# Scores of chunks three to six as products of 64 rows and columns, with k's halves swapped in four heads

## The chip, the cores and the metric

The kernel runs on one core of one Trainium2 chip. The metric is the device time of one execution in microseconds (us). A core has five engines that run their own instruction streams and wait for one another by semaphores: PE (TensorE, matrix products; PEld is its weight load), DVE (VectorE), ACT (ScalarE), POOL (GpSimd) and SP (SyncE), which here issues all DMAs, in order. DMAs run on 16 DMA engines.

## The reference

An mLSTM cell on q, k, v of 4 batches, 8 heads, 768 steps and 40 values per head, then a feed-forward block of 320 to 2,048 to 320 with an exact GELU between:

```python
for t in range(S):
    m_new = np.maximum(f_gate[:, :, t] + m, i_gate[:, :, t])
    f_stab, i_stab = np.exp(f_gate[:, :, t] + m - m_new), np.exp(i_gate[:, :, t] - m_new)
    C = f_stab * C + i_stab * einsum('bhd,bhe->bhde', vt, kt)
    n = f_stab * n + i_stab * kt
    h_tilde = einsum('bhde,bhe->bhd', C, qt)
    y[:, :, t] = sigmoid(o_gate[:, :, t]) * h_tilde / np.maximum(np.abs((n * qt).sum(-1)), 1.0)
h = x @ w_in                      # x: y as 3072 tokens of 320
out = (0.5 * h * (1 + erf(h / sqrt(2)))) @ w_out
```

(The gate's factors are cut here: each holds for a batch and a head.)

## The kernel before

**Tiling.** The 768 steps are cut in six chunks of 128 (`c` = 0 to 5 in the code, chunk one to six in words). Within a chunk, the cell is attention-like: for each batch `b` and head `h`, scores `k q` of 128 key steps (on partitions) by 128 query steps are multiplied by weights `W` (an exponential of gate sums, zero where a key lies after its query), and the product with `v` gives the part of this chunk; what came before enters by a state that is carried from chunk to chunk. A finished chunk of 4 batches is 512 tokens, and goes through the feed-forward block while the next chunk's cell is worked on.

**One cell's steps** (class `Cell`, from L368). `mask` (L378): POOL's affine_select puts 1e30 where the query step comes before the key step, in a tile `W` that a DMA has filled with the gates' running maximum (`load_M`, L154, from the DRAM tile `M_d`). `weights` (L384): ACT takes the exponential for each head, with `aT`, a column per head and key step, as bias; 1e30 becomes zero. `turn_k` and `turn_q`: DVE turns k and q, loaded in blocks by `load_blocks` (L138), into `kT` and `qT`; two heads lie on the two halves of the partitions. `scores` (L469): for each of four pairs of heads and each half `hip`, one fp32 product of 64 rows (40 in use), 128 columns of `kT` and 128 of `qT`, into the PSUM bank of that half (L479); then DVE multiplies each bank into `W` (L482). `carry_two` (L522): products with the state (L531, 64x64 tiles) and, but for the last chunk, what this chunk adds to it (L538, with `kb` and `vw`; `vw` is v times `ewT`, made on POOL at L466). `values` (L564): `W` times `vb` (L573).

`kb` and `vb` hold k and v with key steps on partitions (`load`, L129, one DMA each per cell, L135); from chunk three on `load` is called with 1 and 3, for k and v alone, and with 3 and 4 for the output gate. `aT` and `ewT` come from the gates at the start (`gates_turned`, L215, called by `later_gates`, L276, for the later chunks).

**Order.** It is written out by hand. `FRONT` is a string of steps for the first two chunks and the conversion of the weights; `DOWN` is one for each later chunk's cell among the second products of the chunk before. From chunk three on the cell's scores come in pairs of batches: scores of two batches, `carry_two`, values of two, with feed-forward products between (L768 and L779 up, L844 down). In `FRONT`, the weights arrive as double-precision bits in 26 pieces: `fetch` (L310) loads one on SP, `conv_one` (K, L322) and `conv_two` (J, L340) convert it on DVE and ACT, and `conv_two` fetches the piece four places on, once its buffer is free. `F` is one row of the first chunk's down products (L821), which needs its piece of `w_out`. Letters B are `load_M`, X is `turn_y` (which loads ahead for the cell four places on), R is `split_x`.

Of the kernel before, what the change touches and what calls it, by code (L numbers as in the profile page):

```python
# [9 lines left out]
F32 = mybir.dt.float32  # L10
F32R = mybir.dt.float32r
BF16 = mybir.dt.bfloat16
U32 = mybir.dt.uint32
AF = mybir.ActivationFunctionType
OP = mybir.AluOpType

P = 128
# [11 lines left out]
    I2 O0 g0 L0 P0 L1 E k1 t0 P1 P2 k7 w0 N k2 w1 O1 K L2 Q s0 O3 w2 q D k2 d P3 t1 w3 c0 L3 J v0 t2 K K y0 s1 I7 v1  # L29
    I8 O2 J g1 L4 I5 c1 K I1 I2 y1 s2 x0 t3 B4 O4 B5 g2 J x1 s3 v2 c2 L5 y2 H T0 x2 G0 v3 g3 c3 K y3 M1 J L6 J A x3  # L30
    M0 K W0 O7 K A O6 O5 J M2 W1 S0 C0 K J J T1 U U K L7 V0 K T2 J J A G2 K G1 Y0 W2 S1 K M3 C1 A J S2 J K W3 K V1 C2
    Y1 T3 J J U U S3 V2 K K J G3 J Y2 C3 X0 K V3 J K F J F K K B8 F J K F F J K F F F R0 X1 J J K F J F K X2 F J K F
    J Y3 K F R1 J F Z B9 B10 F X3 R2 Z R3 F"""
DOWN = """
    M0 Z M1 W0 F L3 F B3 W1 Z Z F S0 Z S1 K2 C0 M2 Z G0 G1 G2 G3 V0 Z V1 W2 Z F Q2 K3 Q3 Y0 M3 D3 F F W3 F Z S2 S3
# [4 lines left out]
def kernel(  # L40
# [16 lines left out]
    nc = tc.nc  # L57

    B, H, S, D = q.shape
    L = P  # L60
    NCH = S // L
    NP = H // 2
# [7 lines left out]
    R = P // 2  # L70
# [13 lines left out]
    dram = ctx.enter_context(tc.tile_pool(name="dram", bufs=1, space=bass.MemoryType.DRAM))  # L84
# [12 lines left out]
    ident = const.tile([P, P], F32, name="ident")  # L97
# [3 lines left out]
    aT = const.tile([P, NCH, BH], F32, name="aT")  # L101
    ewT = const.tile([P, NCH - 1, BH], F32, name="ewT")
# [19 lines left out]
    f_sb = gates.tile([BH, NCH, L], F32, name="f_sb")  # L122
    i_sb = gates.tile([BH, NCH, L], F32, name="i_sb")
    M_d = dram.tile([NCH - 1, BH, L], F32, name="M_d")

    def out_of(n):
        return ob[n % NLD].rearrange("p (h d) -> p h d", d=D)

    def load(n, first=0, end=4):  # L129

        if n >= NCH * B:
            return
        c, b = divmod(n, B)
        for src, dst in ((q, qb), (k, kb), (v, vb), (o_gate, None))[first:end]:
            nc.sync.dma_start(out=dst[turn_of(n)][:, :, 0:D] if dst else out_of(n),  # L135
                              in_=src[b, :, c * L:(c + 1) * L, :].rearrange("h p d -> p h d"))

# [12 lines left out]
    def turn_of(n):  # L150

        return n % NLD if n < 2 * B else (n - 2 * B) % NQ
# [19 lines left out]
    for t in vb:  # L172
# [4 lines left out]
                            pattern=[[0, P]], channel_multiplier=1)  # L177
    nc.gpsimd.memset(beyond, 0.0)
    nc.gpsimd.affine_select(out=beyond, in_=beyond, compare_op=OP.is_ge, fill=1.0e30, base=0, pattern=[[1, L]],
                            channel_multiplier=-1)  # L180
# [15 lines left out]
    for j in range(3):  # L196
        m = slice(BH * j, BH * (j + 1))
# [17 lines left out]
    def gates_turned(*parts):  # L215

        for src, dst in parts:
            n = dst.shape[1]
            pg = ps_tr.tile([P, n, BH], F32, name="pg", tag="tr")
            for c in range(n):  # L220
                nc.tensor.transpose(pg[:, c, :], src[:, c, :], ident[0:BH, 0:BH])
            nc.vector.tensor_copy(out=dst, in_=pg)

    def gates_of(c0, c1):

        flat = lambda t: t[:, c0:c1].rearrange("p c l -> p (c l)")
        nc.vector.tensor_tensor_scan(out=flat(bl), data0=flat(keep), data1=flat(f_sb), initial=0.0,
                                     op0=OP.mult, op1=OP.add)
        nc.vector.tensor_tensor(out=a[:, c0:c1], in0=i_sb[:, c0:c1], in1=bl[:, c0:c1], op=OP.subtract)
        for c in range(c0, c1):  # L230
            nc.vector.tensor_tensor_scan(out=M[:, c], data0=a[:, c], data1=a[:, c], initial=m0[:, c:c + 1],
                                         op0=OP.max, op1=OP.max)
            if c + 1 < NCH:
                nc.vector.tensor_tensor(out=m0[:, c + 1:c + 2], in0=bl[:, c, L - 1:L], in1=M[:, c, L - 1:L],
                                        op=OP.add)
# [11 lines left out]
    def decays_turned(e0, e1, g0, g1):  # L247
        e, g = slice(e0, e1), slice(g0, g1)
        gates_turned((ew[:, e], ewT[:, e]), (gg[:, g], gT[:, g]))

    def decays_last(g0, g1):
        g = slice(g0, g1)
        pd = ps_tr.tile([P, g1 - g0, BH], F32, name="pd", tag="tr")
        nc.tensor.matmul(pd.rearrange("p c n -> p (c n)"), last, gT[:, g].rearrange("p c n -> p (c n)"),
                         start=True, stop=True)
        nc.vector.tensor_copy(out=dec[:, g], in_=pd)
# [27 lines left out]
    for name, w in (("in", moe_w_in), ("out", moe_w_out)):  # L284
        rows, cols = w.shape
# [66 lines left out]
    halves = (slice(0, R), slice(R, P))  # L352
# [7 lines left out]
    def unread(bank):  # L360
        for _ in range(idle[0]):
            nc.tensor.matmul(bank, ident, ident, start=True, stop=True, skip_group_check=True)
        idle[0] = 0
# [4 lines left out]
    class Cell:  # L368
# [9 lines left out]
        def mask(self, b):  # L378

            t = Mb[self.c * B + b]  # L380
            nc.gpsimd.affine_select(out=t, in_=t, compare_op=OP.is_ge, fill=1.0e30, base=0,  # L381
                                    pattern=[[0, H], [1, L]], channel_multiplier=-1)

        def weights(self, b):  # L384

# [83 lines left out]
        def scores(self, b):  # L469
            n = self.c * B + b  # L470
            kT, qT = self.kT.pop(b), self.qT[b]

            pool, tag = (ps_tr, "tr") if self.c > 0 and b % 2 else (ps_mm, "a")
            ps = [pool.tile([P, NP, L], F32, name="ps", tag=tag) for hip in range(2)]
            unread(ps[0][:, 0, :])
            for p in range(NP):
                for hip in range(2):
                    r = halves[hip]
                    nc.tensor.matmul(ps[hip][:, p, :], kT[r, p, :], qT[r, p, :], start=True, stop=True)  # L479
            for hip in range(2):  # L480
                w = W[n].rearrange("p (m two) t -> p m two t", two=2)[:, :, hip, :]
                nc.vector.tensor_tensor(out=w, in0=ps[hip], in1=w, op=OP.mult)  # L482
# [75 lines left out]
        def read(self, b):  # L558

            self.reads.append(b)  # L560
            if self.c > 1 and self.reads.count(b) == 2:
                load(self.c * B + b + NQ, 1, 3)
# [77 lines left out]
    w_sums, parts, fars, w_hi, w_lo, w_mid = [], {}, [], [], [], {}  # L640
# [86 lines left out]
    def first_up_steps(h):  # L727

        def step(k):
            ups.append((len(ups) + len(tags_next) % 2, (2 * k, 2 * k + 2, HT * h, HT * h + HT)))  # L730
            if len(ups) == 2:
                first_up()

        return [lambda k=k: step(k) for k in range(HF // 2)]
# [170 lines left out]
    def in_turn(steps):  # L905
        todo = list(steps)
        return lambda: todo.pop(0)() if todo else None

    def cell_steps(c, letters, before=None):
# [8 lines left out]
    n_pieces = range(len(pieces))  # L918
    steps = dict(P=fetch, L=lambda n: load(n, 0, 2), O=lambda n: load(n, 2, 4), B=load_M, E=second_gates, N=later_gates,
                 I=keep_clock, k=warm, D=lambda: decays_turned(0, 2, 0, 1), Q=lambda: decays_turned(2, NCH - 1, 1, NCH - 1),  # L920
                 d=lambda: decays_last(0, 1), q=lambda: decays_last(1, NCH - 1),
                 A=in_turn(first_up_steps(0)), U=in_turn(first_up_steps(1)), F=in_turn(first_down_steps(first_g)),
                 K=in_turn(lambda i=i: conv_one(i) for i in n_pieces), H=products_begin,
                 J=in_turn(lambda i=i: conv_two(i) for i in n_pieces), Z=split_weight)
    steps |= cell_steps(0, "mwgtscvyx") | cell_steps(1, "MWGTSCVYXR")
    play(FRONT, steps)
    for c in range(1, NCH):
# [6 lines left out]
        products, late = down_steps(c, g)  # L934
# [32 lines left out]
```

## Time and profile before

| what | before |
|---|---|
| median of 3 runs | 484.1 us (484.06 to 484.65) |
| profiled execution, its own time | 484.47 us |
| its span (first to last instruction) | 482.7 us |
| PE busy | 473.8 us (98%) |
| DVE busy | 346.4 us (72%) |
| ACT busy | 222.3 us (46%) |
| POOL busy | 69.5 us (14%) |
| granted TensorE clock | 1.0 |
| scores of two batches, chunks three to six | 1.99 us, eight times |

Busy time is a union of the records of an engine. A PE that is busy is not at its peak, since the ends of products are modelled; the starts are measured, so the distance between starts is the better reading. The chain of work that ended last is followed back from the last instruction, at each step to what released it, so a piece on it has no slack by this reading.

### The profile page before, as it was taken

What the parts mean: (1) busy time and instruction counts of PE and PEld (TensorE: products, weight loads), DVE (VectorE), ACT (ScalarE), POOL (GpSimd) and SP (SyncE); (2) the same over time, 40 slices, a digit from 0 to 9 for tenths busy, and PEclk for the clock granted to TensorE, in tenths of its full rate; (3) what the DMA queues carried; (4) which work ended last, traced back from release to release, by engine and by line L of the source; (5) the groups of instructions that cost most, each with busy time, mean ns of one, the idle gap of its engine ahead of it and who ended that gap; (6) DMA issues with size and microseconds to landing.
All of it is one profiled execution on the core that took longest, in us unless ns stands there. A gap on an engine that the chain in (4) does not pass through costs nothing.

```text
span 482.7 us, 11369 instructions
## 1 busy us (share of the span) xinstructions
PE 473.8 (98%) x4484; PEld 413.6 (86%) x4484; DVE 346.4 (72%) x744; ACT 222.3 (46%) x477; POOL 69.5 (14%) x108
## 2 busy tenths in 40 slices
PE   7999999999999999999999999999999999999997
PEld 7788888877777999977999977999977899977997
DVE  7899699898979997747498757498857397724321
ACT  6977999844632941112951113961103852112300
POOL 3001200001000234200144200145000212000000
PEclk9999999999999999999999999999999999999999
DMA  9998955379320365921264922265921250100001
GB/s 174 202 220 180 208 145 140 90 184 218 104 27 7 36 126 76 206 50 22 31 117 72 216 50 25 29 127 75 205 49 22 32 90 3 47 9 0 1 1 54
DMA packets 168021, 44.28 MB, mean 92 GB/s; under 512 B 154176, under 2 KB 161504, under 8 KB 167968
## 3 DMA queue, kind: packets, MB, share of 16 engines
q1 hardware_dynamic: 167968, 43.56, 46.4%
q8 instruction: 35, 0.57, 0.5%
q14 instruction: 18, 0.15, 0.1%
HBM read 39.52 MB, written 4.01 MB: 90 GB/s over the span
## 4 chain that ended last, share of the span: by engine, by line
PE 91%; DVE 4%; SPq 1%; ACT 1%; DMA 1%; issue 1%; DVEq 0%
PE po L844 32%; PE pu L768 21%; PE po L821 7%; PE pu L713 6%; PE pu L779 6%; PE ph L573 5%; PE ps L479 5%; PE pf L531 2%; PE pu L719 2%; PE px L608 2%; PE pf L538 1%; SPq L135 1%; PE pt L453 1%; ACT g L783 1%; PE pf L498 1%; DMA ob<-in_o_gate_dram 1%
## 5 line engine op out<-in xcount | busy, mean ns | idle before, releaser
L844 PE MATMUL po<-w_out,g 128*128 128x160 f32 x640 | 91.2, 300 | 0.0
L844 PEld LDWEIGHTS po<-w_out,g 128*128 128x128 f32 x640 | 87.8, 190 | 1.8 <-ACT g L783 1.8
L783 ACT ACTIVATE g<-pu 128x512 f32<-128x512 f32 x80 | 40.8, 616 | 53.5 <-PE pu L779 53.3
L844 PE MATMUL po<-w_sums,sums 128*128 128x160 f32 x320 | 47.2, 302 | 0.0
L844 PEld LDWEIGHTS po<-w_sums,sums 128*128 128x128 f32 x320 | 44.2, 190 | 0.4
L618 ACT ACTIVATE x_hi<-px 128x384 fp32r<-128x384 f32 x20 | 9.8, 489 | 70.6 <-PE px L608 70.6
L768 PE MATMUL pu<-x_hi,w_in_hi 128*128 128x512 f32 x160 | 41.7, 402 | 0.0
L700 DVE TENSOR_TENSOR sums<-g 128x512 f32<-128x512 f32 x20 | 13.8, 689 | 38.6 <-ACT g L783 38.6
L768 PE MATMUL pu<-x_lo,w_in_lo 128*128 128x512 f32 x160 | 40.7, 396 | 0.0
L407 ACT ACTIVATE W<-W,aT 128x128 f32<-128x128 f32 x128 | 39.1, 389 | 0.4 <-POOL W L381 0.2
L482 DVE TENSOR_TENSOR W<-ps,W 128x512 f32<-128x512 f32 x40 | 25.5, 685 | 15.9 <-ACT W L407 10.9
L768 PEld LDWEIGHTS pu<-x_hi,w_in_hi 128*128 128x128 f32 x160 | 28.5, 188 | 9.4 <-ACT g L783 4.1
L768 PEld LDWEIGHTS pu<-x_lo,w_in_lo 128*128 128x128 f32 x160 | 30.1, 188 | 7.2
L821 PE MATMUL po<-w_out,g 128*128 128x320 f32 x128 | 35.3, 434 | 0.0
L857 DVE TENSOR_TENSOR o_sb<-po,o_sb 128x320 f32<-128x320 f32 (+1 forms) x27 | 12.6, 465 | 28.9 <-PE po L844 24.8
L821 PEld LDWEIGHTS po<-w_out,g 128*128 128x128 f32 x128 | 24.0, 190 | 9.8 <-DVE w_out L348 0.2
L768 PE MATMUL pu<-x_all,w_in_mid 128*128 128x512 f32 x80 | 31.7, 396 | 0.1
L783 ACT ACT_TABLE_LOAD x5 | 6.4, 1283 | 55.1 <-DMA blocks<-in_k_dram 27.5
L768 PE MATMUL pu<-x_all,w_mid 128*128 128x512 f32 x80 | 31.7, 396 | 0.0
L419 POOL MEMSET g<- 32x1024 f32 x8 | 7.6, 944 | 155.8 <-ACT W L407 155.6
L713 PE MATMUL pu<-first_x,w_in 128*128 128x256 f32 x128 | 28.9, 382 | 0.0
L381 POOL TENSOR_SCALAR_AFFINE_SELECT W<-W 128x1024 f32<-128x1024 f32 x16 | 18.1, 1137 | 67.3 <-DMA W<-M_d 58.9
(180 smaller groups left out, 907.8 us busy)
## 6 DMA issues: line engine op xcount, KB each, us to landing
W<-M_d SPq DMA_DIRECT2D x16, 512.0 KB, 5.7
bits<-in_moe_w_in_dram SPq DMA_DIRECT2D x20, 256.0 KB, 4.1
bits<-in_moe_w_out_dram SPq DMA_DIRECT2D x16, 320.0 KB, 3.6
ob<-in_o_gate_dram SPq DMA_DIRECT2D x24, 160.0 KB, 3.9
out_dram<-o_sb SPq DMA_DIRECT2D x24, 160.0 KB, 1.9
vb<-in_v_dram SPq DMA_DIRECT2D x22, 160.0 KB, 5.1
kb<-in_k_dram SPq DMA_DIRECT2D x22, 160.0 KB, 4.8
g<-M_d SPq DMA_DIRECT2D x4, 512.0 KB, 4.2
```

Source lines behind the costliest of these rows:

```text
L381: nc.gpsimd.affine_select(out=t, in_=t, compare_op=OP.is_ge, fill=1.0e30, base=0, pattern=[[0, H], [1, L]], channel_multiplier=-1)
L407: nc.scalar.activation(out=W[n][:, h, :], in_=src, func=AF.Exp, scale=-1.0, bias=aT[:, self.c, r:r + 1])
L479: nc.tensor.matmul(ps[hip][:, p, :], kT[r, p, :], qT[r, p, :], start=True, stop=True)
L482: nc.vector.tensor_tensor(out=w, in0=ps[hip], in1=w, op=OP.mult)
L573: nc.tensor.matmul(ph[r, h, :], Pm[:, h, r], vb[turn_of(n)][:, h, :], start=True, stop=True)
L700: nc.vector.tensor_tensor(out=s1, in0=a21, in1=a22, op=OP.add)
L713: nc.tensor.matmul(banks[-1][e][:, i - i0, :], in_tile(i, x)[:, e, i % 2 * P:(i % 2 + 1) * P], first_x[:, x, t0:t1], start=(x == 0 and i = ...
L768: nc.tensor.matmul(pus[i][e], w[k][:, e, i * P:(i + 1) * P], x[:, k, :], start=(n == 0 and k == 0), stop=False, skip_group_check=True)
L779: nc.tensor.matmul(pu[e], w[r, i // 2, i % 2 * P:(i % 2 + 1) * P], x[r, NX, :], start=False, stop=(n == 2), skip_group_check=True)
L783: nc.scalar.activation(out=g.t[:, HF * e + i, :], in_=pu[e], func=AF.Gelu, scale=4097.0)
L821: nc.tensor.matmul(po[b], g.t[:, f, b * L:(b + 1) * L], w_out[:, f, :], start=(f == 0), stop=(f == NF - 1))
L844: nc.tensor.matmul(bank[at][:, i, :], lhs(j, t), rhs(j), start=(first and i == 0 and j == 0), stop=(i == n - 1 and j == HF - 1), skip_grou ...
```

## The change

For chunks three to six (`self.c` of 2 and more) the scores of a batch are made from products of 64 rows and 64 columns. Of the 128x128 block of key and query steps, the quarter with late keys and early queries is masked. A product for the early 64 keys takes all 128 queries, one for the late 64 keys the late 64 queries alone. For heads 0 to 3 the early keys' results go to partitions 0 to 63; for heads 4 to 7 to partitions 64 to 127, so that the four kinds of products (two halves of partitions in, two out) have equal work. What has key steps on partitions must then have its halves swapped for heads 4 to 7: k and v in `kb` and `vb` (three DMAs in place of one), and `aT` and `ewT`, which six new DMAs take to DRAM and back, at two new letters in `FRONT`: r (`halves_out`) and p (`halves_back`). The mask is set in three parts. The quarter that no product writes is zeroed in PSUM by four bfloat16 products of a zero block of the identity, 64 rows by 64 columns by 128, ahead of the scores.

A batch has sixteen fp32 products of scores for eight, and four bfloat16 products more.

```diff
--- before.py
+++ after.py
@@ -29,7 +29,7 @@
     I2 O0 g0 L0 P0 L1 E k1 t0 P1 P2 k7 w0 N k2 w1 O1 K L2 Q s0 O3 w2 q D k2 d P3 t1 w3 c0 L3 J v0 t2 K K y0 s1 I7 v1
     I8 O2 J g1 L4 I5 c1 K I1 I2 y1 s2 x0 t3 B4 O4 B5 g2 J x1 s3 v2 c2 L5 y2 H T0 x2 G0 v3 g3 c3 K y3 M1 J L6 J A x3
     M0 K W0 O7 K A O6 O5 J M2 W1 S0 C0 K J J T1 U U K L7 V0 K T2 J J A G2 K G1 Y0 W2 S1 K M3 C1 A J S2 J K W3 K V1 C2
-    Y1 T3 J J U U S3 V2 K K J G3 J Y2 C3 X0 K V3 J K F J F K K B8 F J K F F J K F F F R0 X1 J J K F J F K X2 F J K F
+    Y1 T3 J J U U S3 V2 K K J G3 J Y2 C3 X0 K V3 J K F J F K K B8 r F J p K F F J K F F F R0 X1 J J K F J F K X2 F J K F
     J Y3 K F R1 J F Z B9 B10 F X3 R2 Z R3 F"""
 DOWN = """
     M0 Z M1 W0 F L3 F B3 W1 Z Z F S0 Z S1 K2 C0 M2 Z G0 G1 G2 G3 V0 Z V1 W2 Z F Q2 K3 Q3 Y0 M3 D3 F F W3 F Z S2 S3
@@ -122,6 +122,7 @@
     f_sb = gates.tile([BH, NCH, L], F32, name="f_sb")
     i_sb = gates.tile([BH, NCH, L], F32, name="i_sb")
     M_d = dram.tile([NCH - 1, BH, L], F32, name="M_d")
+    swapped_d = [dram.tile([P, n * B, H // 2], F32, name=f"swapped{n}") for n in (NCH - 2, NCH - 3)]
 
     def out_of(n):
         return ob[n % NLD].rearrange("p (h d) -> p h d", d=D)
@@ -132,6 +133,13 @@
             return
         c, b = divmod(n, B)
         for src, dst in ((q, qb), (k, kb), (v, vb), (o_gate, None))[first:end]:
+            if dst and n >= 2 * B:
+                x, to = src[b, :, c * L:(c + 1) * L, :].rearrange("h p d -> p h d"), dst[turn_of(n)][:, :, 0:D]
+                h0, h1 = slice(0, H // 2), slice(H // 2, H)
+                nc.sync.dma_start(out=to[:, h0], in_=x[:, h0])
+                for i in range(2):
+                    nc.sync.dma_start(out=to[halves[i], h1], in_=x[halves[1 - i], h1])
+                continue
             nc.sync.dma_start(out=dst[turn_of(n)][:, :, 0:D] if dst else out_of(n),
                               in_=src[b, :, c * L:(c + 1) * L, :].rearrange("h p d -> p h d"))
 
@@ -221,6 +229,20 @@
                 nc.tensor.transpose(pg[:, c, :], src[:, c, :], ident[0:BH, 0:BH])
             nc.vector.tensor_copy(out=dst, in_=pg)
 
+    def later_heads():
+        return [t[:, 2:].rearrange("p c (b h) -> p (c b) h", h=H)[:, :, H // 2:] for t in (aT, ewT)]
+
+    def halves_out():
+
+        for t, t_d in zip(later_heads(), swapped_d):
+            nc.sync.dma_start(out=t_d, in_=t)
+
+    def halves_back():
+
+        for t, t_d in zip(later_heads(), swapped_d):
+            for i in range(2):
+                nc.sync.dma_start(out=t[halves[i]], in_=t_d[halves[1 - i]])
+
     def gates_of(c0, c1):
 
         flat = lambda t: t[:, c0:c1].rearrange("p c l -> p (c l)")
@@ -378,8 +400,13 @@
         def mask(self, b):
 
             t = Mb[self.c * B + b]
-            nc.gpsimd.affine_select(out=t, in_=t, compare_op=OP.is_ge, fill=1.0e30, base=0,
-                                    pattern=[[0, H], [1, L]], channel_multiplier=-1)
+            if self.c < 2:
+                parts = ((t, 0),)
+            else:
+                parts = ((t[:, 0:H // 2], 0), (t[0:R, H // 2:], -R), (t[R:P, H // 2:, 0:R], 0))
+            for x, base in parts:
+                nc.gpsimd.affine_select(out=x, in_=x, compare_op=OP.is_ge, fill=1.0e30, base=base,
+                                        pattern=[[0, x.shape[1]], [1, x.shape[2]]], channel_multiplier=-1)
 
         def weights(self, b):
 
@@ -473,10 +500,19 @@
             pool, tag = (ps_tr, "tr") if self.c > 0 and b % 2 else (ps_mm, "a")
             ps = [pool.tile([P, NP, L], F32, name="ps", tag=tag) for hip in range(2)]
             unread(ps[0][:, 0, :])
-            for p in range(NP):
-                for hip in range(2):
-                    r = halves[hip]
-                    nc.tensor.matmul(ps[hip][:, p, :], kT[r, p, :], qT[r, p, :], start=True, stop=True)
+            if self.c < 2:
+                products = [(slice(0, P), p, slice(0, P), slice(0, P)) for p in range(NP)]
+            else:
+                products = [(halves[x ^ y], y * NP // 2 + p, halves[x], slice(R * x, P))
+                            for p in range(NP // 2) for x in range(2) for y in range(2)]
+                for x in range(2):
+                    for hip in range(2):
+                        zero = ident[halves[hip], R * (1 - hip):R * (1 - hip) + R].bitcast(BF16)
+                        nc.tensor.matmul(ps[hip][halves[x], (1 - x) * NP // 2:(2 - x) * NP // 2, 0:R], zero[:, 0:R],
+                                         zero.rearrange("p (m t) -> p m t", t=R), start=True, stop=True)
+            for rows, p, s_half, t in products:
+                for r, bank in zip(halves, ps):
+                    nc.tensor.matmul(bank[rows, p, t], kT[r, p, s_half], qT[r, p, t], start=True, stop=True)
             for hip in range(2):
                 w = W[n].rearrange("p (m two) t -> p m two t", two=2)[:, :, hip, :]
                 nc.vector.tensor_tensor(out=w, in0=ps[hip], in1=w, op=OP.mult)
@@ -918,7 +954,7 @@
     n_pieces = range(len(pieces))
     steps = dict(P=fetch, L=lambda n: load(n, 0, 2), O=lambda n: load(n, 2, 4), B=load_M, E=second_gates, N=later_gates,
                  I=keep_clock, k=warm, D=lambda: decays_turned(0, 2, 0, 1), Q=lambda: decays_turned(2, NCH - 1, 1, NCH - 1),
-                 d=lambda: decays_last(0, 1), q=lambda: decays_last(1, NCH - 1),
+                 d=lambda: decays_last(0, 1), q=lambda: decays_last(1, NCH - 1), r=halves_out, p=halves_back,
                  A=in_turn(first_up_steps(0)), U=in_turn(first_up_steps(1)), F=in_turn(first_down_steps(first_g)),
                  K=in_turn(lambda i=i: conv_one(i) for i in n_pieces), H=products_begin,
                  J=in_turn(lambda i=i: conv_two(i) for i in n_pieces), Z=split_weight)
```

## The prediction

> **What bounds the kernel now.** I read the page first: busy time by engine, the DMA queues, the chain of work that ended last.
>
> ```profile
> span 482.7 us, 11369 instructions
> ...
> PE 473.8 (98%) x4484; PEld 413.6 (86%) x4484; DVE 346.4 (72%) x744; ACT 222.3 (46%) x477; POOL 69.5 (14%) x108
> ...
> q8 instruction: 35, 0.57, 0.5%
> ...
> PE 91%; DVE 4%; SPq 1%; ACT 1%; DMA 1%; issue 1%; DVEq 0%
> ```
>
> TensorE is the bound: time cut from its stream counts in full unless something else becomes late. The q8 row is used below: 35 packets of 16 KB for TensorE's 9,040 records, so 256 instructions in a packet.
>
> Next the chain in order of time, in the chunk that the change touches first (start, length, what; a fp32 product makes two pieces):
>
> ```profile
> 164.61 1.99 PE ps L479 x32
> 166.60 1.07 PE pf L531 x64
> 167.67 1.06 PE pf L538 x32
> 168.73 1.87 PE ph L573 x64
> ...
> 183.61 1.22 PE ph L573 x41
> 184.83 0.90 issue
> 185.73 0.90 PE ph L573 x23
> ```
>
> Scores of two batches (L479) take 1.99 us, eight times from chunk 3 on: 15.9 us is all that the new products can shorten. The 0.90 us of "issue" is a halt for which no engine is the cause; it returns below.
>
> What tiles do in parallel stands in the rows of the two lines (weight load and product: count, ns, shape rows*columns):
>
> ```profile
> L479 PE MATMUL ps<-qT,kT x384: 269/272/373, 15.4 to 400.2; 64*128 64x128 f32 x192
> ...
> L531 PE MATMUL pf<-state,qT x512: 227/227/248, 166.5 to 401.3; 64*64 64x41 f32 x171
> ```
>
> Single records of L479 start every 112 ns on each of two row halves. Those of L531 start every 58 ns on each of four 64x64 tiles, the four some 7 ns apart: four weight loads really run at once. [...]
>
> Last, VectorE where w_out's last two rows are converted (L331 begins a piece, L348 ends it):
>
> ```profile
> 118.60 0.32 DVE L331 TENSOR_SCALAR pow<-bits 128x320 uint32<-128x320 uint32 x1
> ...
> 120.67 0.49 DVE L348 SCALAR_TENSOR_TENSOR w_out<-sig,pow 128x320 f32<-128x320 f32 x1
> ...
> 125.96 0.49 DVE L348 SCALAR_TENSOR_TENSOR w_out<-sig,pow 128x320 f32<-128x320 f32 x1
> ```
>
> TensorE's last L821 row starts at 126.50 and needs the piece that ends at 126.45: no slack there.
>
> [...] from L844 (one tile) to L479 the stream stops for 0.09 us, from L479 to L531 for 0.09, between types in one mode not at all. [...] the halt at 184.83 falls at record 3,521; the packet for it started at 182.78, 1.2 us after the block ahead of it began at 181.56 (k and v loads held the DMA engines), ended at 184.25, and TensorE went on at 185.73. [...] 8 to 32 KB loads land 2.0 to 2.2 us after issue.
>
> **The change, part by part.**
>
> Products. Before, from the end of L844's stream (164.45) to the end of L531's (167.48): 3.03 us. After: switch 0.09, zero's weight load 0.03; per batch four bf16 zeros of 128 columns in parallel on four tiles, 0.06 (bf16 at this size starts every 55 ns at L402), then on each tile two products with 128 columns and two with 64, each in two passes: 4 x 112 + 4 x 58 = 680 ns. L531 then follows in the same mode, its switch and first load hidden: 0.91. Sum 0.12 + 2 x 0.74 + 0.91 = 2.51. The order of the column halves flips at each step; starts in order cost about 13 ns at each of six flips: 0.08. Gain 0.44 a pair, eight pairs: 3.5 us. Ends: 4.2 if flips are free and types mix freely, 1.2 if every zero group stops the stream for 0.09 on both sides.
>
> Instruction blocks. 40 more TensorE instructions per batch (32 for eight more fp32 products, eight for the zeros) make the stretch of a pair 464 instead of 384, in 5.4 us instead of 6.0. Counting instructions from the halt (blocks start at 3,520 plus or minus multiples of 256) puts the block starts in the eight pairs at +91, +3, +176, +88, +5, +173, +90 and +70 instructions; before they lay at +80 to +91 (the last at +144), in L531's beginning. The 256 instructions that follow then take, at the rates of the four lines (scores 96 per us, L531 137, L538 60, L573 68): 2.65, 2.3, 3.1, 2.6, 2.3, 3.15, 2.65, 2.5 us. Before they took 3.0 at the least. What a fetch needs, from that trace: packet start 0.2 us after the block's (calm cases -0.3 to 0.7), 1.05 for the packet (0.93 to 1.4), 1.34 afterwards (the least that went without a halt; 1.48 at the halt): 2.6. [...] the packet starts some 0.6 later: 3.2. Halts: 0.55, 0.1, 0.6, 0.55, 0.7, 0.1 for the first, third, fourth, seventh, eighth, sixth: 2.6. The second keeps its 0.9, since its crossing lies in slow L844 but among the same loads; the fifth has none. Ends: 0 [...] and 5.
>
> Front. After the W load at 103.78, two more DMAs carry aT and ewT of heads 4 to 7 out (r), 2,048 and 1,536 pieces of 16 bytes; one fetch later four bring them back swapped (p). 32-byte packets of L145 took 9 ns each, so 7,168 pieces on 16 engines are 4.0 us of DMA time; written to DRAM in 16 bytes they may take double. p waits for r's landing, and SP is in order (and each DMA waits for the one eight issues before it): behind p stand the fetches of w_out's pieces 13 to 15 and k, v and the gate. r goes behind W (its packets end at 107.0), lands at 109.8 to 111; four issues of 0.45 put the fetch that went at 108.38 to 112.0. Then k and v, six DMAs for two (1.8 more), put the one of 111.50 to 115.6; k, v and gate packets are ahead of it, landing about 120.2. VectorE took that piece at 118.60: 1.6 late, and all of its work slides, so w_out's last row slides from 126.45 to 128.05 and TensorE's last L821 with it. Ends: 0 if r lands by 108, 3.5.
>
> Loads later. Four more issues per batch, about 0.45 us each on SP. blocks of the next chunk land 17 us ahead of L430, W loads and gates further; these cost nothing. Only k and v of batch 4 are near: in chunk 3 they land at 180.8, POOL weighs v until 181.68, L538 needs it at 183.0. Data, not issue, bounds that landing (512-byte packets of M ahead), so it moves by 0.5 while TensorE comes 0.5 sooner: about 0.3 with what queues behind POOL's vw (the state's decays). Without that cover up to 1.3.
>
> Masks. 128x1024 took 1.09 us on POOL; the three parts have 512, 512 and 256 elements in a partition, 1,280 for 1,024, so 1.4 and two more starts, some 1.5. POOL is 14% busy; ScalarE can begin after the first part, 0.5 us sooner. Nothing, save that L482 in the last chunk comes within 0.1 us of L573. These small ones: 0.5 in all, 0 to 1.5.
>
> Sum: -3.5 + 2.6 + 1.6 + 0.5 = +1.2. Against the profiled execution (484.47, 1.8 around its span) 485.7; the median of the runs is 0.37 lower: 484.1 + 1.2 = **485.3 us**.
>
> **Rivals.** (1) Blocks arrive in time: -3.5 + 1.6 + 0.3 gives 482.5, and 480.8 with r early as well. For it: seven dense pairs of before show no halt. Against: their least slack was 1.34 us after the packet with 3.0 us to spend, and now 2.3 to 2.65. It decides where a fetch needs under 2.5 us. This one is faster. (2) SP's chain and the 16-byte DMAs are worse, as written in small pieces, or the zeros stop the stream: front 3.5, halts 3, gain 2.5: 488. Against: the DMA engines have room at 107 to 110. (3) The tiles don't do what is meant: two of four 64x64 products with 128 columns at once, 8 x 112 + 8 x 58 = 1.36 us for 0.89 a batch: 16 x 0.5 + 2 = 494. L531's four loads in 58 ns speak against it. (4) The terms cancel: 484.1.
>
> **How the numbers follow.** The forecast 0.47 (its own range 484.3 to 487), rival 1 0.27, rival 2 0.14, rival 3 0.05, rival 4 0.07. A change within 0.2%, 0.97 us, can't be told from none. Faster: 0.22 (most of rival 1). Same: 0.22 (0.10 of the forecast, 0.05 of rival 1, rival 4). Slower: 0.56. The range 481.4 to 488.4 leaves out the lower end of rival 1, the upper part of rival 2 and rival 3.
>
> **What would show it.** The pairs' scores in the chain near 1.55 us instead of 1.99, L531 near 0.93: right on the products. New "issue" pieces of 0.4 to 1 us inside L531 to L573: right on blocks; none: rival 1. L821's last row at about 128 and waits of VectorE's L331 for bits near 119: right on the front. A zero product with 0.09 us on either side, or a pair over 1.9, makes me wrong on the products; a wait of L538 for POOL over 1 us, on the loads.

## The result, and the profile after

| what | before | after |
|---|---|---|
| median | 484.08 us (4 runs, 483.96 to 484.65) | 497.58 us (4 runs, 497.11 to 500.04) |
| ratio | | 1.0287, 95% interval 1.0252 to 1.0321 |
| span of the profiled execution | 482.7 us | 495.8 us |
| first product of L768 (after: L804) behind the front | 128.5 us | 142.7 us |
| the eight pairs' stretches, summed | 49.0 us | 48.1 us |
| rest of the span | 305.2 us | 305.0 us |

The last three rows add up to the span. A pair's stretch runs from the start of the last L844 product (after: L880) ahead of its scores to the start of the next one behind its values. Medians here count every execution, but ratios leave out slow ones, over 1.5% above the fastest of their kernel (three each of the whole-rows and on-chip kernels below). The forecast was 485.3 us with a range of 481.4 to 488.4: slower was right, the size was not. All of the loss lies in the front, +14.2 us. The new products and their halts together gain 0.9 us.

The page of the kernel after (busy time, the queue of instructions, the chain by engine):

```profile
span 495.8 us, 12213 instructions
...
PE 477.1 (96%) x4804; PEld 413.7 (83%) x4804; DVE 343.1 (69%) x744; ACT 222.6 (45%) x477; POOL 80.7 (16%) x140
...
q8 instruction: 38, 0.62, 0.6%
...
PE 80%; DVE 8%; DMA 6%; SPq 2%; ACT 2%; issue 1%; DVEq 0%
```

Before, PE was 91% of that chain and DMA 1%. Three more packets of instructions are fetched (q8). What the DMA share is, the chain in order of time shows in the front (start, length, what):

```profile
102.80 0.42 SPq L173
...
103.27 15.48 DMA swapped<-aT
...
118.78 0.57 SPq L244
...
122.62 3.62 DMA bits<-in_moe_w_out_dram
...
127.71 3.98 DMA bits<-in_moe_w_out_dram
...
133.80 0.49 DVE w_out L370
...
138.98 4.11 PE po L857 x8
```

Step r stores 32 KB of `aT` to DRAM and takes 15.5 us to land. SP stands in front of p (L244) until then, and the fetch of w_out that went out at 108.38 before goes at 122.62. The conversion of a w_out piece that started at 120.67 before starts at 133.80 here, and the last piece is ready at 138.93 for 126.45: 12.5 of the 14.2 us.

The other 1.7 us are TensorE's last row (L857). From its first product to the front's end it takes 3.71 us here and 2.02 before. The windows view of that row before, and of all but the row's first 0.3 us after (busy time by engine, then the granted clock, the DMA share and GB/s):

```profile
126.50:128.52 2.02, 2.02 (x9) 1.47 (x9) 2.02 (x5) 1.85 (x5) 0.00 (x0) 1.00 0.46 77
```

```profile
139.24:142.64 3.40, 3.40 (x7) 2.06 (x7) 3.40 (x7) 1.59 (x4) 2.09 (x3) 0.50 0.51 133
```

The granted clock is half from 139.2 to 142.6, after TensorE had stood waiting for w_out's pieces. The prediction had no term for this. Two more such stretches, from 122.2 and 129.0, end while TensorE still waits for a piece, and cost nothing.

The chain in order of time in pair six:

```profile
338.74 0.18 PE ps L511 x4
338.92 0.67 PE ps L515 x32
339.58 0.06 PE ps L511 x4
339.64 0.67 PE ps L515 x32
340.31 0.92 PE pf L567 x64
341.23 1.06 PE pf L574 x32
342.29 1.28 PE ph L609 x43
343.56 1.53 issue
345.10 0.83 PE ph L609 x21
```

The scores of a pair (L511 and L515) take 1.58 us for 1.99, and the products with the state (L567) 0.92 for 1.07. "issue" is the halt that the prediction spoke of. It lies where a new block of 256 instructions begins (427 records into the pair; here 38 packets of 16 KB carry 9,680 records), and the packet that fetches the block started 2.3 us after the block ahead of it had begun. (The lengths of halts below are the distance from one start to the next, some 0.2 us more than the "issue" piece: 1.76 us here.) From the trace's packets, some of the quarter microseconds before it, and what the DMA engines were given in them:

```
us       pieces started in 0.25 us, bytes: number
339.75   160: 74    4096: 7
340.25              4096: 25      (the block ahead begins at 340.29)
340.75              4096: 18
341.25   160: 32    4096: 17
341.75   160: 291   4096: 3
342.25   160: 253
342.50   160: 220   16384: 1     (the packet of instructions)
```

The pieces of 4,096 bytes are a load of M (`load_M`, 512 KB), those of 160 bytes are k and v. In pair eight, where nothing is loaded, the packet started 0.3 us after the block ahead.

### The profile page after: what moved, and what is told of

It is laid out like the page before. It is cut to its first block, busy times and chain, and to the rows that moved or that the text cites. A ratio compares the mean times of both kernels' runs of the same rounds, so it can differ in the third digit from the quotient of the medians.

```text
span 495.8 us, 12213 instructions
## 1 busy us (share of the span) xinstructions
PE 477.1 (96%) x4804; PEld 413.7 (83%) x4804; DVE 343.1 (69%) x744; ACT 222.6 (45%) x477; POOL 80.7 (16%) x140
## 4 chain that ended last, share of the span: by engine, by line
PE 80%; DVE 8%; DMA 6%; SPq 2%; ACT 2%; issue 1%; DVEq 0%
PE po L880 31%; PE pu L804 21%; PE pu L749 6%; PE pu L815 6%; PE ph L609 4%; PE ps L515 3%; DMA swapped<-aT 3%; PE pu L755 2%; DMA bits<-in_moe_w_out_dram 2%; PE pf L567 1%; PE px L644 1%; PE pf L574 1%; SPq L143 1%; PE po L857 1%; PE pt L480 1%
## 5 line engine op out<-in xcount | busy, mean ns | idle before, releaser
L880 PE MATMUL po<-w_out,g 128*128 128x160 f32 x640 | 91.2, 300 | 0.0
L880 PEld LDWEIGHTS po<-w_out,g 128*128 128x128 f32 x640 | 87.8, 190 | 1.8 <-ACT g L819 1.8
L857 PE MATMUL po<-w_out,g 128*128 128x320 f32 x128 | 41.1, 481 | 7.3 <-DVE w_out L370 7.3
L880 PE MATMUL po<-w_sums,sums 128*128 128x160 f32 x320 | 47.2, 302 | 0.0
L880 PEld LDWEIGHTS po<-w_sums,sums 128*128 128x128 f32 x320 | 44.2, 190 | 0.4
L857 PEld LDWEIGHTS po<-w_out,g 128*128 128x128 f32 x128 | 26.6, 212 | 20.1 <-DVE w_out L370 9.0
L804 PE MATMUL pu<-x_hi,w_in_hi 128*128 128x512 f32 x160 | 41.7, 402 | 0.0
L804 PE MATMUL pu<-x_lo,w_in_lo 128*128 128x512 f32 x160 | 40.6, 396 | 0.0
L408 POOL TENSOR_SCALAR_AFFINE_SELECT W<-W 128x512 f32<-128x512 f32 (+3 forms) x40 | 26.2, 671 | 71.8 <-DMA W<-M_d 64.3
L804 PEld LDWEIGHTS pu<-x_hi,w_in_hi 128*128 128x128 f32 x160 | 28.5, 188 | 9.5 <-ACT g L819 4.1
L804 PEld LDWEIGHTS pu<-x_lo,w_in_lo 128*128 128x128 f32 x160 | 30.1, 188 | 7.2
L804 PE MATMUL pu<-x_all,w_in_mid 128*128 128x512 f32 x80 | 31.7, 396 | 0.1
L804 PE MATMUL pu<-x_all,w_mid 128*128 128x512 f32 x80 | 31.7, 396 | 0.0
L355 ACT ACTIVATE pow<-pow,e_hi 128x320 f32<-128x320 uint32 (+1 forms) x26 | 16.1, 620 | 29.9 <-DVE pow L353 29.9
```

Of the source, the lines that this page charges most:

```text
L355: nc.scalar.activation(out=p, in_=pu, func=AF.Relu, scale=-I23, bias=e_hi)
L408: nc.gpsimd.affine_select(out=x, in_=x, compare_op=OP.is_ge, fill=1.0e30, base=base, pattern=[[0, x.shape[1]], [1, x.shape[2]]], channel_m ...
L804: nc.tensor.matmul(pus[i][e], w[k][:, e, i * P:(i + 1) * P], x[:, k, :], start=(n == 0 and k == 0), stop=False, skip_group_check=True)
L857: nc.tensor.matmul(po[b], g.t[:, f, b * L:(b + 1) * L], w_out[:, f, :], start=(f == 0), stop=(f == NF - 1))
L880: nc.tensor.matmul(bank[at][:, i, :], lhs(j, t), rhs(j), start=(first and i == 0 and j == 0), stop=(i == n - 1 and j == HF - 1), skip_grou ...
```

## The experiments

Four questions: which part of the trip through DRAM costs 14 us; whether the twelve additional loads do; what sets the halts; and what the products are worth without either. Each run is compared with runs of the kernel before on its own chip. For the profiled execution of each, in us:

| kernel | median | front ends | stretches | rest |
|---|---|---|---|---|
| before | 484.08 | 128.5 | 49.0 | 305.2 |
| after | 497.58 | 142.7 | 48.1 | 305.0 |
| before + trip | 495.57 | 140.2 | 48.5 | 305.0 |
| after, whole rows stored | 486.20 | 128.3 | 49.0 | 308.1 |
| after, swapped on the chip | 487.24 | 129.9 | 49.8 | 307.6 |
| before + split loads | 485.01 | 128.4 | 50.9 | 305.1 |
| after, read back late | 496.74 | 139.9 | 48.9 | 306.1 |
| whole rows, 36 records more | 493.31 | 131.9 | 51.9 | 307.7 |
| whole rows, no M | 482.45 | 130.3 | 46.7 | 305.0 |
| after, 32-byte pieces | 484.23 (one run) | 129.6 | 47.8 | 305.0 |
| after, 16-byte pieces apart | 490.22 (one run) | 134.4 | 49.1 | 305.0 |
| whole rows, M later | 481.61 | 128.5 | 45.8 | 305.0 |
| before, M later | 483.77 | 130.3 | 48.5 | 305.1 |

Three fronts hold something of their own: read back late, no M, and before with M later had TensorE's clock at half from 15.3 to 18.8 us in their profiled executions, which the others had not. The last two have their last piece of w_out at 128.2 for 126.45.

**Before with the trip alone.**

```diff
...
+    def halves_out():
+        for t, t_d in zip(later_heads(), swapped_d):
+            nc.sync.dma_start(out=t_d, in_=t)
+    def halves_back():
+        for t, t_d in zip(later_heads(), swapped_d):
+            for i in range(2):
+                nc.sync.dma_start(out=t[halves[i]], in_=t_d[halves[i]])
...
-    K K B8 F J K F F
+    K K B8 r F J p K F F
```

> The kernel before with nothing but the trip of a and e through DRAM added at its two places, the halves put back where they came from. Theory A (the 14 us are made by storing 16-byte pieces to DRAM: the pieces trickle out, the fetch queued behind them on the same DMA engines trickles with them, and SP stands before the read back): first product of the block after the front at 142 to 144 us instead of 128.9, median 484.1 + 14 = 498 (496 to 500). Rival B (the front is late because of the twelve additional loads of k and v and SP's issues, the trip being only a part): 486 to 491.

Measured: 495.57 us (4 runs), ratio 1.0233 (1.0214 to 1.0252), front at 140.2. So the trip alone makes 11.7 of the 14.2 us, and rival B falls. Of the other 2.5 us, 1.7 are the half clock in the last row: here the row takes 2.02 us at full clock. The last piece of w_out is 0.8 us earlier here, at 138.17 for 138.93. After p, the next fetch but one goes at 125.77 here and at 127.71 in the kernel after, where six loads of k and v (L139, L141) lie before it in place of two; that they make the 0.8 us is argued, not tried.

**Whole rows to DRAM, the same reads back.**

```diff
-        for t, t_d in zip(later_heads(), swapped_d):
-            nc.sync.dma_start(out=t_d, in_=t)
+        for t, t_d in zip((aT, ewT), swapped_d):
+            nc.sync.dma_start(out=t_d, in_=t[:, 2:])
```

(Not shown: the DRAM tiles are made to hold whole rows, and the read back picks heads 4 to 7 out of them.)

> The changed kernel with the same trip through DRAM, but stored as whole rows of 512 and 384 bytes; it is read back in the same four issues of 16-byte pieces, swapped. The counts of issues, the place of the wait on SP and TensorE's instructions stay. Theory A: the store lands about 2.5 us after its issue, the front ends at 129 to 131 us, median 497.6 - 13 = 484.6 (483.3 to 486.5). Rival C (the wait of SP before the read back, or 16-byte pieces in either direction, whatever is stored): over 491.

Measured: 486.20 us (18 runs), ratio 1.0022 (0.9998 to 1.0046), front at 128.3. The DMA view (KB each, median us from issue to landing), of this kernel and of the kernel after:

```profile
swapped<-aT SPq DMA_DIRECT2D x1, 64.0 KB, 3.8
...
aT<-swapped SPq DMA_DIRECT2D x2, 16.0 KB, 2.6
```

```profile
swapped<-aT SPq DMA_DIRECT2D x1, 32.0 KB, 15.5
```

Twice the bytes land in a quarter of the time, and reading back in 16-byte pieces takes 2.6 us. With that the whole front's loss is gone: not the wait before p, nor the issues, nor small pieces as such, but storing 16-byte pieces to DRAM. The time was 1.6 us over theory A's figure, and its single runs lie between 482.4 and 492.2. The rest of the span says why: 308.1 for 305.0. The windows view around pair four, in steps of 5 us and then in two of 3.41:

```profile
250.00:255.00 5.00, 4.99 (x180) 4.71 (x179) 4.21 (x10) 2.36 (x8) 2.98 (x6) 1.00 0.86 178
255.00:260.00 5.00, 3.23 (x67) 3.15 (x67) 3.00 (x10) 0.00 (x0) 2.54 (x5) 0.86 0.35 45
260.00:265.00 5.00, 5.00 (x31) 5.00 (x31) 2.14 (x3) 0.00 (x0) 1.07 (x2) 0.80 0.34 35
265.00:270.00 5.00, 5.00 (x40) 5.00 (x39) 4.48 (x16) 0.49 (x1) 0.00 (x0) 1.00 0.78 172
```

```profile
255.21:258.62 3.41, 1.85 (x63) 1.85 (x62) 2.29 (x8) 0.00 (x0) 1.21 (x3) 1.00 0.35 48
258.63:262.04 3.41, 3.41 (x18) 3.33 (x15) 0.50 (x1) 0.00 (x0) 2.25 (x3) 0.50 0.31 32
```

Pair four halts 2.0 us at 255, and from 258.63 to 262.04 TensorE is granted half its clock; 0.86 and 0.80 are the means of wider windows that hold a part of it. The same follows pair six's halt of 1.7 us. Two falls, 3.1 us. The unprofiled runs agree: the six of this kernel with a mean granted clock of 0.999 or 1.0 took 482.4 to 485.0 us, the other twelve, at 0.982 to 0.996, 485.5 to 492.2.

**The swap on the chip.**

```diff
-    nc.vector.tensor_copy(out=dst, in_=pg)
+    for c in range(n):
+        for i in range(2):
+            nc.tensor.matmul(ph[halves[i], c, :], src[:, c, halves[1 - i]], ident[0:BH, 0:BH], start=True, stop=True)
+    nc.vector.tensor_copy(out=heads(dst)[:, :, 0:H // 2], in_=heads(pg)[:, :, 0:H // 2])
+    nc.vector.tensor_copy(out=heads(dst)[:, :, H // 2:], in_=heads(ph)[:, :, H // 2:])
...
-    K K B8 r F J p K F F
+    K K B8 F J K F F
```

> The changed kernel without the trip through DRAM: the swapped halves are made by 14 more small products on TensorE where a and e are turned, and four VectorE copies in place of two. k and v are still loaded swapped, in three issues each. The 56 instruction records that this adds move all blocks of 256 records 56 places earlier in the later code. Theory A with halts like those of the changed kernel: front ends at 129 to 130 us, median 497.6 - 14.2 + 0.2 = 483.6 (482.3 to 485). Pairs two and five (blocks then start at -55 and -53) have no halt, pairs one, three, four, six and seven (+33, +118, +30, +115, +32) have one of 0.3 to 1.8 us. Rival B (additional loads of k and v hold the front): 488 or more.

Measured: 487.24 us (19 runs), ratio 1.0039 (1.0017 to 1.0060), front at 129.9. The front's loss is gone here too, without any trip. The list of halts was half wrong. Pair three halted (0.3 us) and pair five did not, as expected, and pair six halted 2.4. But pairs one, four and seven, with a block start at +30 to +33, had none; pair two, with one at -55, halted 2.4 us, at the third start. Both long halts were again followed by a fall of the clock.

**Before with split loads.**

```diff
-    nc.sync.dma_start(out=to, in_=x)
+    nc.sync.dma_start(out=to[:, h0], in_=x[:, h0])
+    for i in range(2):
+        nc.sync.dma_start(out=to[halves[i], h1], in_=x[halves[i], h1])
```

(`to` and `x` stand for the tile and the source of k or v.)

> The kernel before with k and v of chunks three to six loaded in three issues each instead of one, into the same places. Theory A: SP has slack there, the front ends within 1 us of 128.9 and the stretches keep their length, median 484.1 to 485.1. Rival B (the additional issues hold the fetches of w_out back): 487 to 492.

Measured: 485.01 us (20 runs), ratio 1.0013 (1.0000 to 1.0026), front at 128.4. SP has room for them. Against the expectation the stretches did not keep their length: they are 1.8 us longer in the profiled execution, all of it halts (pair two 1.6 for 1.1, pair four 1.1, pair six 0.3).

**The read back at the end of the front.**

```diff
-    K K B8 r F J p K F F
+    K K B8 r F J K F F
...
-    X3 R2 Z R3 F
+    X3 R2 Z R3 F p
```

> The changed kernel with its trip through DRAM stored in 16-byte pieces as it is, but the four issues that read it back moved from behind the next F and J to the very end of the front, so that SP doesn't stand before them while the store lands. Compared with the kernel that stores whole rows (486.2 us). If the standing of SP is all: front ends at 128 to 130 us, about 486. If the pieces also clog the DMA engines: the fetch of w_out issued at about 107 still lands at about 119 us and those issued on time behind it land at 120 to 122, front ends at 131 to 137, median 488 to 494. If the place of the wait does not matter: front at 141 to 143, about 497.

Measured: 496.74 us (4 runs), ratio 1.0233 (1.0202 to 1.0264), front at 139.9. None of the three cases held as written: most of the loss stays though SP no longer stands before p. The last piece of w_out is ready at 137.81, for 138.93 in the kernel after. Against the 128.2 of the two other kernels with an early fall of the clock that is 9.6 us late, where the kernel after is 12.5. The chain of this kernel has the cause:

```profile
108.77 15.69 DMA bits<-in_moe_w_out_dram
...
124.48 0.34 DVE pow L353
```

The fetch of w_out itself takes 15.7 us, for 2.9 to 4.1 at this place in the kernel before (12.8 in the kernel after): it was issued 2.9 us after the second store, in the same queue (q1). I had let the later fetches land at 120 to 122; the next one of the chain goes out at 126.86. This run shows the wait behind the stores in their own queue, 15.7 us, and nothing of other queues.

**Pieces of 32 bytes, and 16-byte pieces set apart.** Both stores have the 3,584 pieces of the kernel after, 64 bytes from one to the next in DRAM.

```diff
-    swapped_d = [dram.tile([P, n * B, H // 2], F32, name=f"swapped{n}") for n in (NCH - 2, NCH - 3)]
+    swapped_d = [dram.tile([P, n * B, 2 * H], F32, name=f"swapped{n}") for n in (NCH - 2, NCH - 3)]
...
-            nc.sync.dma_start(out=t_d, in_=t)
+            nc.sync.dma_start(out=t_d[:, :, 0:H], in_=t)
```

That is the 32-byte one, where `t` holds all eight heads of a batch. The 16-byte one has `t_d[:, :, 0:H // 2]` and heads 4 to 7.

> The changed kernel with the same 3,584 pieces in its store to DRAM, each of 32 bytes instead of 16 (both halves of the eight heads, set apart by 32 bytes so that they don't join). The read back takes the same 16-byte halves. If the price is by piece: the store of a lands 15 us after its issue as in the changed kernel, front ends at 141 to 144 us, about 497. If it is by byte: lands after 25 us or more, over 504. If 32-byte pieces are stored at the 9 ns of 32-byte loads that the prediction used: lands after about 5 us, front at 128 to 131 us, 485 to 488.

> The changed kernel with its store of 16-byte pieces, each piece now 64 bytes after the one before it in DRAM instead of 16. The kernel with 32-byte pieces 64 bytes apart was quick, the changed kernel with 16-byte pieces side by side slow: size and distance both differed. If the size makes it slow: the store of a lands about 15 us after its issue, front ends at 141 to 144, about 497. If it is the neighbours in the same 32 or 64 bytes, stored by other DMA engines at the same time: lands after about 5 us, front at 128 to 131, 484 to 487.

Measured in one run each: 484.23 us with 32 bytes (front at 129.6), 490.22 with 16 bytes apart (front at 134.4). The DMA views, first of 32 bytes, then of 16 apart:

```profile
swapped<-aT SPq DMA_DIRECT2D x1, 64.0 KB, 5.2
...
swapped<-ewT SPq DMA_DIRECT2D x1, 48.0 KB, 5.6
```

```profile
swapped<-aT SPq DMA_DIRECT2D x1, 32.0 KB, 8.5
swapped<-ewT SPq DMA_DIRECT2D x1, 24.0 KB, 9.5
```

So it is neither a price by piece nor one by byte. The same number of pieces lands after 5.2 us with 32 bytes, 8.5 with 16 bytes apart and 15.5 with 16 bytes side by side: the second run's two cases are both part of it. Size and spacing both count; why they do, no view shows.

**36 records more in the front**, on the kernel that stores whole rows.

```diff
-    warm(6)
+    for _ in range(15):
+        nc.tensor.matmul(cold[:, 0:51], w_out[:, 0, 0:P], w_out[:, 0, 0:51], start=True, stop=True, skip_group_check=True)
```

> The kernel that stores whole rows, with 36 more instruction records at 1 us of the program (fifteen warming products of 51 columns for six of 128, the same columns in all). It moves all blocks of 256 records 36 places earlier: the starts in pairs one to eight go from 89, 1, 174, 86, 3, 171, 88, 68 to 53, -35, 138, 50, -33, 135, 52, 32. Theory (a halt comes at the second block start of a pair when the first lies at about 60 to 180): pairs two, five and eight have none, pairs one, four and seven at most 0.3 us, pairs three and six 0.3 to 2.5; sum 1.5 to 3.5 us against 5.4, median 482 to 484.5. Rival (the place in the pair does not matter): sum 4 to 6 us, median about 486.

Measured: 493.31 us (4 runs), ratio 1.0174 (1.0158 to 1.0191). This failed as an experiment on time: short products start no faster here than long ones, every 0.21 us, so the warming lasts until 7.6 us instead of 3.9, and the front ends 3.6 us later. The clock also fell after pairs four and six (means of 0.54 and 0.78 from 260 to 270 us, 0.89 and 0.77 from 335 to 345). Of the halts it tells something. Pairs two, five and eight had none, as expected; pair three had 0.35 and pair six 1.8. Pairs one, four and seven, at +50 to +53, had 0.8, 1.8 and 1.3 us where I had allowed 0.3.

Over the nine kernels with the new products that the table holds, counting halts of over 0.2 us: where a block starts between -35 and +33 records of a pair's first product, none of 21 pairs halted; where one starts between +50 and +176, 41 of 49 did; of two with one at -55 and -53, one did. The place goes with whether there is a halt, and hardly with how long it is.

**No loads of M**, on the kernel that stores whole rows. The weights of chunks three to six leave M out.

```diff
-            nc.sync.dma_start(out=to, in_=src.unsqueeze(0).to_broadcast([P, H, L]))
+            nc.gpsimd.memset(to, 0.0)
...
+        if n >= 2 * B:
+            nc.gpsimd.memset(Mb[n], 0.0)
+            return
         nc.sync.dma_start(out=Mb[n].rearrange("p h l -> p (h l)"),
                       in_=src.rearrange("h l -> (h l)").unsqueeze(0).to_broadcast([P, H * L]))
```

> The kernel that stores whole rows, without the loads of M of chunks three to six: GpSimd clears these tiles instead, so the weights leave M out. The 512 KB that each of these loads moves falls away, the instructions of TensorE and their blocks stay. Theory (a halt is long when the fetch of instructions lies behind such a load on the DMA engines, and the TensorE clock falls after a long halt): pairs four and six, 2.0 and 1.7 us, go to 0.7 or less, no fall of the clock after them, median 486.2 - 2.3 - 3 = 481 to 483.5. Rival (the latency of the fetch is its own): halts of 1.5 to 2 us stay, 485 to 487.

Measured: 482.45 us (6 runs), ratio 0.9953 (0.9913 to 0.9992). Pair four halts 0.8 instead of 2.0 us, pair six 1.0 instead of 1.7, a little over the 0.7 expected; the clock falls after neither, and the rest of the span is 305.0. So 1.2 of pair four's 2.0 us and 0.7 of pair six's 1.7 come from M's loads, which the DMA engines have to carry before the packet of instructions.

**M later**, on the kernel that stores whole rows, and on the kernel before. Nothing is left out.

```diff
     def values(self, b):
-            if self.c > 1 and b > 0:
-                load_M(n + NW)
     def finish(self, b):
...
             self.finished.append(b)
+            if self.c > 1 and b > 0:
+                load_M(n + NW)
```

> The kernel that stores whole rows, with three of each chunk's four loads of M (512 KB each) issued where the heads are finished instead of where the values are multiplied, so that they move after the second pair's products and not in front of its fetch of instructions. Nothing is left out. Theory (the long halts are fetches that lie behind these loads): pairs four and six halt 0.5 to 1.1 us instead of 2.0 and 1.7, the clock does not fall after them, median 481.5 to 483.5, faster than the kernel before. Rival (the loads of k and v behind them take their place): halts of 1.4 to 2 us, 485 to 487.

> The kernel before with the same move of M's loads and nothing else. Its halt in pair two (1.1 us, with the block at the same place in all eight pairs) is cut if it is due to a load of M: 483 to 484. Rival: it stays, 484.4. The difference to the run above is what the products of 64 rows are worth with both rid of these loads: theory 0.5 us a pair less 0.3 to 0.5 us of halt a pair, 0.5 to 2.5 us in all.

Measured: 481.61 us (9 runs, 480.67 to 483.25), ratio 0.9933 (0.9907 to 0.9959), 0.7% faster than the kernel before; and 483.77 us (22 runs), ratio 0.9974 (0.9954 to 0.9994), for the kernel before with the move. Page and chain (pair four) of the first:

```profile
span 479.3 us, 12217 instructions
...
PEclk9999999999999999999999999999999999999999
```

```profile
253.94 1.06 PE pf L574 x32
255.00 0.11 PE ph L609 x2
255.11 0.25 issue
255.36 2.06 PE ph L609 x62
```

```profile
255.00:260.00 5.00, 4.75 (x83) 4.59 (x82) 3.13 (x11) 0.00 (x0) 3.59 (x6) 1.00 0.35 48
260.00:265.00 5.00, 5.00 (x40) 5.00 (x39) 4.72 (x11) 0.49 (x1) 0.05 (x1) 1.00 0.38 39
```

Pair four's "issue" is 0.25 us (1.78 with M's load in front), and the last two lines are the windows whose mean clock was 0.86 and 0.80. Pair two of the kernel before keeps a trace of its halt (its stretch is 6.40 us, 7.36 before, 6.22 without any), and pair eight has a new one of 0.5. With M out of the way of both, the change with whole rows is worth 483.77 - 481.61 = 2.2 us; in the stretches of the two profiled executions it is 48.5 - 45.8 = 2.7.

## Why the prediction was wrong, point by point

**Front: chain right, price wrong, and this is the failed step.** The chain was the one described: r's pieces, p's wait, the fetches behind it on SP, VectorE's last conversions, L821's last rows. But the step "32-byte packets of L145 took 9 ns each, so 7,168 pieces on 16 engines are 4.0 us of DMA time; written to DRAM in 16 bytes they may take double" took its price from loads into SBUF, and the doubling from no trace. Measured, r's 3,584 pieces take from the first packet at 105.8 to the second store's landing at 119.6: 13.7 us, or 61 ns for each of an engine's 224. With 32 bytes the same count takes 16 ns each (106.3 to 109.9). A warning: the packets of 16 bytes still show a median of 9 ns in the trace. The price isn't in their durations but in the gaps between them and in the landing: the last one starts at 112.8. The term was +1.6 with an upper end of 3.5; it measured +14.2, of which 12.5 are the late pieces of w_out and 1.7 the half clock that followed the wait for them.

Two smaller parts of that step were wrong too. It held that w_out's later pieces had no slack, 1.6 us late at VectorE and at the end. With whole rows the last fetch goes out 3.6 us later than before (116.05 for 112.43), and the front ends where it did (128.3 for 128.5). And it made SP's order the carrier of the delay (in the trace of before none of SP's 420 issues starts ahead of the landing of the one eight before it); the run with the late read back shows that without SP's wait before p some 9.6 of the 12.5 us stay (an estimate, from 137.81 - 128.2).

**Products: right in kind, too small.** Forecast 3.5 us, 0.44 a pair. A pair without halts is 5.65 us long for 6.22, and 4.77 for 5.28 in chunk six: 6 x 0.57 + 2 x 0.51 = 4.4 us. From the last L844 start to the last L531 start the traces have 3.13 us before and 2.56 after: 0.57 gained, where the forecast had 3.03 - 2.51 - 0.08. So what it took off for the flips in the order of column halves (0.08 a pair, my estimate) didn't show, and the new stretch is 0.05 shorter than it counted. The zeros start 0.08 us ahead of the first score, and the stream doesn't stop between the types (45 to 70 ns from the last zero's start to the first score's), as forecast. Rival 3, tiles not in parallel, falls: by it the scores of a pair would take 2.7 us, and they take 1.58.

**Instruction blocks: right in place and kind, a little small.** The forecast block starts (+91, +3, +176, +88, +5, +173, +90, +70) came at +89, +1, +174, +86, +3, +171, +88, +68. Halts came in pairs one, three, four, six, seven and eight, all at the second start. Pair two lost its halt, against the forecast. Against pairs without halts, the stretches hold 48.1 - (6 x 5.65 + 2 x 4.77) = 4.7 us of halts, before 49.0 - (6 x 6.22 + 2 x 5.28) = 1.1: +3.6 for +2.6. What was missed is the length where loads are under way: pair six was given 0.1 us and halted 1.8, pair four 0.6 and halted 1.4, pair three 0.1 and 0.4, while pairs one, seven and eight halted 0.3 to 0.4 where 0.55 to 0.7 was given. The forecast let the packet start 0.8 us after the block ahead began (0.2 from the trace of before, 0.6 my estimate for denser code, which no trace had shown); in pairs six and four it started 2.3 and 1.4 after, in pair eight 0.3.

**Loads later and masks.** Given 0.5; the rest of the span is 0.2 us shorter, so nothing measurable. POOL's busy time rose by 11 us, and no stage became longer for it.

**The sum.** -4.4 + 3.6 + 14.2 - 0.2 = +13.2, against +13.1 in the spans. Without the front the forecast had -0.4 and the spans have -1.1. That these lie so close is luck: the products gained 0.9 us more than forecast and the halts took 1.0 more. Rival 2 (488) named the right place, "as written in small pieces", and was stopped at 3.5 us by the same price.

**What the runs add.** Stored in whole rows, the change is no gain either (1.0022, interval 0.9998 to 1.0046): in its profiled execution the 4.4 us of gain go into halts, and the long ones end in falls of the clock. Rival 1, blocks in time, had 482.5, and with M's loads moved too the time is 481.6; but blocks are still late there, by 0.3 to 0.6 us in five pairs.

## What to carry to other kernels

Price a small store to DRAM by a store of that size and spacing, not by a load: with whole rows in place of 16-byte pieces the whole loss of the front was gone, and a fetch queued behind the slow store waited too (12.8 and 15.7 us for 2.9 to 4.1). When code for TensorE gets denser, count its instructions per block, and look at which transfers are under way where the next block is fetched; moving three of each later cell's loads of M (512 KB each) behind the values took 4.6 us off the kernel with the denser code (486.2 to 481.6) and 0.8 off the kernel before. And where a halt or a wait has grown, look at the granted clock behind it, in windows narrow enough to show its true value, before the halt is called the whole loss.

## What the runs showed of the hardware that was not expected

- 3,584 pieces stored to DRAM: the first store of them lands 15.5 us after its issue with 16 bytes side by side, 8.5 with 16 bytes 64 apart, 5.2 with 32 bytes 64 apart; 3.8 when the same columns go in rows of 512 bytes. Reading 16-byte pieces back took 2.4 to 5.4 us.
- A w_out fetch of 320 KB issued behind the slow store took 15.7 us, for 2.9 to 4.1 at this place in the kernel before.
- Packets of instructions started late with data under way on the DMA engines: in pair six of the kernel after 2.3 us behind the start of the block ahead, among pieces of M, k and v; in pair eight, where nothing is loaded, 0.3. In pairs four and six the halts were 1.1 to 2.4 us with M's loads where they were (seven kernels; pair four of the on-chip kernel had none), 0.3 to 1.0 without them.
- The granted clock fell after 7 of the 10 halts of over 1.6 us in these profiled executions, and after none of the shorter ones. The falls are to half. They last 3.41 us (258.63 to 262.04 in the whole-rows kernel) or, behind pair four of the kernel with 36 records more, about twice that. Length alone doesn't sort the halts: in windows of 5 us TensorE stood 1.43 us around pair six of the whole-rows kernel, with a fall, and 2.01 around pair four with 16 bytes apart, without one. In the kernel after, the clock changes at 122.17, 125.58, 128.99, 132.41, 139.23 and 142.65, each 3.41 us or twice that behind the one before. Counted on in steps of 3.41 us, an estimate, 344.04 lies inside pair six's halt: TensorE stood 0.48 us of the step ahead of it and 1.06 of the step behind, and no fall followed. In the whole-rows kernel it stood 1.56 us (3.41 less 1.85 busy) of the 3.41 us up to 258.62, and the fall came there. Two cases show no rule. The two falls of the whole-rows kernel cost 3.1 us in the rest of the span, for an estimate of 1.7 each from half of 3.41.
